# Two-sided decode attention: one whole-tile V slot and a mixed P·V product instead of two half slots

## The chip, the cores and the metric

The kernel runs on one core of a Trainium2 chip. The metric is device time in microseconds from one launch; a time here is the median of runs of the same program, and lower is better. The core has five engines: TensorE (PE, matrix products), VectorE (DVE, elementwise and reductions), ScalarE (ACT, activations), GpSimd (POOL) and SyncE (SP, here only a queue that issues loads). Sixteen DMA engines move data from HBM to on-chip memory.

## The reference

Two attention decode steps for a single token are computed side by side and concatenated. Each has 32 heads of 128, 32 key/value heads (no sharing), a cache of 16384 positions and a model width of 512, all in bfloat16.

```python
q = (x @ wq).reshape(B, Sq, Hq, Dh).transpose(0, 2, 1, 3)
scores = einsum("bhqd,bhkd->bhqk", q, k) * (Dh ** -0.5)
p = softmax(scores)
o = einsum("bhqk,bhkd->bhqd", p, v)
return o.transpose(0, 2, 1, 3).reshape(B, Sq, Hq * Dh) @ wo
```

Side A uses all 16384 positions of K and V. Side B uses the last 4096 of each head (a window). With one query row, every K and V element is read once and used once: 268 MB of K and V for A, 67 MB for B, and 17 MB of weights.

## The kernel before

**Steps.** The heads are worked through in 20 steps, `T` = 0 to 19, listed in `steps`. Sixteen belong to A (two heads each, 64 partitions per head, 256 positions per partition) and four, at `T` = 0, 7, 13 and 19, to B (eight heads in two windows of four heads, 128 positions per partition). Each step needs one K tile and one V tile of 128 partitions x 256 positions x 128, that is 64 KB per partition, 8.39 MB. Half a tile, 128 positions and 32 KB per partition, is called `u` = 0 or 1.

**Scores on VectorE.** `scores_prod` (L200) multiplies a half K tile by the query in place; `scores_tree` folds the 128 products of each position to 8 in four additions (L207) and reduces these to one score (L213). `unit_max` (L218, L220) takes the largest score per partition and turns it into a row by a PE transpose; `max_all` (L225, L229, L232) reduces that to a maximum per head and spreads it back over partitions.

**Softmax on ScalarE.** `soft` takes the exponential (L240), writes one copy of the probabilities per head masked to that head's partitions (`pm`, L248), and `soft_sum` and `recip` form the sums and their reciprocals.

**P·V on TensorE.** `pv` multiplies with the probabilities as the stationary operand, 8 or 16 columns wide, and 4 positions of V, 512 columns, as the moving one (L292): 64 matmuls per A tile. Row c of the result is good only in its own block of 128 columns. `evict` scales it to on-chip memory (L308), and `columns` picks the good blocks into columns with four small fp32 products (L323) and copies them into `O` (L327). Step NT - 3 and the last step use another form, `pv_columns` (L338): V itself is stationary, one position at a time, and the probabilities are 2 or 4 moving columns, so that the result is a column at once; `scale_columns` (L353) scales it on VectorE.

**Buffers and the order of loads.** Two pools hold the large tiles: `kring`, two slots of a whole K tile, and `vring`, two slots of half a V tile. SP issues nearly all loads, in program order, and waits in that order until the slot of a load is free. In step T it issues `load_v(T-1, 0)`, `load_k(T+1)`, and `load_v(T-1, 1)`; TensorE does `pv(T-2, 1)` and then `pv(T-1, 0)` in the same step. A's K rows are 64 KB, its V rows 32 KB; all of B's are 32 KB. At the start the two `wq` weights use the V slots; at the end the `wo` weights use a K slot and a V slot. The order of instructions on each engine is that of the program (`manual_schedule`): nothing is moved by a scheduler.

**Start.** `x` is loaded transposed, 128 partitions of 4 elements of 2 bytes (L417), and `spread_x` spreads it over masked columns; `project_q` forms the queries on PE.

**End.** `permute_o` reorders the columns of `O`. `project_out_rows` (L373) forms A's output with 32 matmuls of 512 columns. B's `wo` is loaded in four pieces (`wo_pieces`), and `project_out_columns` works them as they come: wo stationary for the first three (L393), and the last two rows of wo through `spread_o` with wo as the moving operand (L406). The result goes out from L412.

Of the kernel before, what the change touches and what calls it, by code (L numbers as in the profile page):

```python
# [11 lines left out]
P = 128  # L12
# [13 lines left out]
def kernel(  # L26
# [26 lines left out]
    vring = ctx.enter_context(tc.tile_pool(name="vring", bufs=2))  # L53
# [10 lines left out]
    def vslot(name):  # L64
        return vring.tile([P, CH, DH], BF16, tag="vring", name=name)
# [3 lines left out]
    one_f = singles.tile([1, 1], F32, tag="one_f")  # L69
    ones_col = singles.tile([P, 1], F32, tag="ones_col")  # L70
# [53 lines left out]
    def load_v(T, u, dst=None, pieces=1):  # L124
        s, g = steps[T]
        V[T, u] = vslot("vt") if dst is None else dst
        n = CH // pieces
        for k in range(pieces):
            if s is A:
                src = a_pair(A_v_cache, g)[:, u * CH : (u + 1) * CH, :].rearrange("p l d -> p (l d)")  # L130
            else:
                src = b_window(B_v_cache, 2 * g + u)
            nc.sync.dma_start(
                out=V[T, u][:, k * n : (k + 1) * n, :].rearrange("p l d -> p (l d)"),
                in_=src[..., k * n * DH : (k + 1) * n * DH],
            )

    def load_wq(s):
        s.wq_t = vslot("wqt")
        nc.sync.dma_start(  # L140
            out=s.wq_t[:, :, :].rearrange("p a b -> p (a b)").rearrange("p (c f) -> p c f", c=KC),
            in_=s.wq.rearrange("(p c) f -> p c f", c=KC),
        )
# [12 lines left out]

    def spread_x(s, flat):
        s.xb = flat[:, 0 : s.nh * KC * P].rearrange("p (h c m) -> p h c m", h=s.nh, c=KC)
        nc.vector.memset(s.xb, 0.0)
        for j in range(s.nh):  # L160
# [7 lines left out]
    def project_q(s):  # L168
        wq = s.wq_t[:, :, :].rearrange("p a b -> p (a b)").rearrange(
# [13 lines left out]
    class Unit:  # L183
        def __init__(self, T, u):
            self.T = T
            self.s, g = steps[T]
            self.col = self.s.nh * g if self.s is A else self.s.nh * (2 * g + u)
            self.n = 2 * CH if self.s is A else CH
            self.rows = 4 * self.s.nh
            self.split = T == NT - 3  # L190
            self.last = self.split or T == NT - 1
            self.sc = one.tile([P, 2 * CH], F32, tag="sc", name="sc")

# [8 lines left out]
    def scores_tree(T, u):  # L202
        s, g = steps[T]
# [5 lines left out]
        if s is B or u == 0:  # L209
            units[T, u] = Unit(T, u)  # L210
        un = units[T, u if s is B else 0]
        c0 = u * CH if s is A else 0
        nc.vector.tensor_reduce(out=un.sc[:, c0 : c0 + CH], in_=k[:, :, 0:8], axis=AX.X, op=ALU.add)  # L213
        return un if s is B or u == 1 else None

    def unit_max(un):
        m = small.tile([P, 1], F32, tag="m", name="m")
        nc.vector.tensor_reduce(out=m[:, :], in_=un.sc[:, 0 : un.n], axis=AX.X, op=ALU.max)  # L218
        un.sm = ps_m.tile([P, 512], F32, tag="sm", name="sm")
        nc.tensor.transpose(un.sm[0:1, 0:P], m[:, :], identf[:, :])  # L220

    def max_all(un):
        s = un.s
        M = small.tile([1, 4], F32, tag="M", name="M")
        nc.vector.tensor_reduce(  # L225
            out=M[:, 0 : s.nh], in_=by_head(s, un.sm[0:1, 0:P]), axis=AX.X, op=ALU.max
        )
        Mr = one.tile([1, P], F32, tag="Mr", name="Mr")
        nc.vector.tensor_copy(  # L229
            by_head(s, Mr[:, :]), M[:, 0 : s.nh].unsqueeze(2).broadcast_to([1, s.nh, P // s.nh])  # L230
        )
        nc.tensor.matmul(un.sm[:, 128:129], lhsT=Mr[:, :], rhs=one_f[:, :], start=True, stop=True)  # L232

    def soft(un):
        s = un.s
        bias = small.tile([P, 1], F32, tag="bias", name="bias")
        nc.scalar.activation(out=bias[:, :], in_=un.sm[:, 128:129], func=ACT.Copy, scale=-inv)  # L237
        p = one.tile([P, 2 * CH], BF16, tag="p", name="p")
        cs = small.tile([P, 1], F32, tag="cs", name="cs")
        nc.scalar.activation(  # L240
            out=p[:, 0 : un.n], in_=un.sc[:, 0 : un.n], func=ACT.Exp, scale=inv, bias=bias[:, :],
            accum_out=cs[:, :],
        )
        un.cs = cs
        pm = small.tile([P, 4 * CH], BF16, tag="pm", name="pm")
        un.pm = pm[:, 0 : un.n * s.nh].rearrange("p (i h c) -> p i h c", h=s.nh, c=4)
        for j in range(s.nh):
            nc.scalar.activation(  # L248
                out=un.pm[:, :, j, :], in_=p[:, 0 : un.n].rearrange("p (i c) -> p i c", c=4),
# [3 lines left out]
        if un.last:  # L253
            un.csm = small.tile([P, 4], F32, tag="csm", name="csm")
            nc.scalar.activation(
                out=un.csm[:, 0 : s.nh], in_=s.mask[:, :], func=ACT.Copy, scale=un.cs[:, :]
            )

    def soft_sum(un):
        s = un.s  # L260
        if un.last:
            nc.tensor.matmul(
                un.sm[:, 136 : 136 + s.nh], lhsT=ones_col[:, :].broadcast_to([P, P]),
                rhs=un.csm[:, 0 : s.nh], start=True, stop=True,
            )
        else:
            nc.tensor.matmul(
                un.sm[0 : un.rows, 136:137], lhsT=s.rows[:, :, :].rearrange("p a b -> p (a b)"),
# [264 lines left out]
```

## Time and profile before

| | |
|---|---|
| median of 3 runs | 828.04 us (827.94 to 828.24) |
| the profiled execution's own time | 828.17 us |
| its span, first to last instruction | 826.4 us |
| busy: DVE / PE / ACT | 761.6 / 387.3 / 67.1 us |
| moved by the load queue | 352.33 MB |
| mean rate over the span | 427 GB/s |
| mean granted TensorE clock | 0.704 of full |

The profile page gives busy time per engine, the load queues with the share of 16 engines' span that their packets took, and the chain of work that ended last: followed back from the last instruction, at each step to what released it. Lines of a timeline are: start in us, duration, engine, source line, operation, what it writes and reads, a count, and in brackets how long the engine was idle before and what ended that. PE is a matmul, PEld the loading of its stationary operand, SPq the issue of a load. Lines of windows give, for a stretch of time, its length, then the busy time and count of PE, PEld, DVE, ACT and POOL, then the granted TensorE clock, the DMA share, and GB/s.

### The profile page before, as it was taken

The page shows a single profiled execution, that of the slowest core. Times are in us where ns is not written, and L with a number is a line of the kernel's source. Part 1 is how long each engine was busy: PE and PEld are TensorE (multiplying, and loading weights), DVE is VectorE, ACT ScalarE, POOL GpSimd, SP SyncE. Part 2 cuts the span into 40 slices and gives each one's busy share as a digit, 9 for nine tenths or more (in the row PEclk, how much of TensorE's full clock was granted, in tenths as well). Part 3 has the DMA queues.
Part 4 walks back from the last instruction along what each step waited for, and adds up shares of the span by engine and source line. Part 5 has one row for each costly group of instructions (what it writes and reads, how often), then busy time and mean ns, then how long its engine had stood idle before and what let it go on. Part 6 is the DMA issues. An engine that isn't in the chain of part 4 may idle for free.

```text
span 826.4 us, 4998 instructions
## 1 busy us (share of the span) xinstructions
PE 387.3 (47%) x2100; PEld 172.3 (21%) x2100; DVE 761.6 (92%) x363; ACT 67.1 (8%) x194; POOL 0.7 (0%) x6
## 2 busy tenths in 40 slices
PE   3405062708172645536180817354453617180884
PEld 1101021303031212212030302121221203030444
DVE  1899999999999999999999999999999999999930
ACT  0110010101000001101010100010010101010110
POOL 0000000000000000000000000000000000000000
PEclk9766577768585858677675858586766767585695
DMA  9999999999999999999999999999999999999996
GB/s 381 431 431 432 429 435 428 435 427 438 446 416 431 431 446 420 440 423 437 423 439 430 437 425 431 440 428 446 416 444 420 447 416 447 415 431 431 429 424 289
DMA packets 10688, 352.64 MB, mean 427 GB/s; under 512 B 1449, under 2 KB 1450, under 8 KB 1706
## 3 DMA queue, kind: packets, MB, share of 16 engines
q1 hardware_dynamic: 10376, 352.33, 99.1%
q8 instruction: 16, 0.26, 0.1%
q10 hardware_dynamic: 290, 0.00, 0.0%
q14 instruction: 6, 0.05, 0.0%
HBM read 352.32 MB, written 0.00 MB: 426 GB/s over the span
## 4 chain that ended last, share of the span: by engine, by line
DVE 79%; DMA 18%; PE 2%; issue 1%; ACT 0%; DVEq 0%; ACTq 0%; SPq 0%
DVE kt L200 36%; DVE kt L207 35%; DMA kt<-in_A_k_cache_dram 10%; DVE sc L213 5%; DMA wot<-in_B_wo_dram 4%; DMA xTA<-in_A_x_dram 3%; DMA vt<-in_A_v_cache_dram 2%; PE o L292 1%; DVE m L218 1%; DVE Mr L229 1%; DVE M L225 0%; PE ocol L338 0%; PE out_cols L393 0%; DVE r L277 0%; PE out_rows L406 0%
## 5 line engine op out<-in xcount | busy, mean ns | idle before, releaser
L207 DVE TENSOR_TENSOR kt<-kt 128x8192 bf16<-128x8192 bf16 (+3 forms) x160 | 344.9, 2156 | 4.7
L292 PE MATMUL o<-vt,pm 128*8 128x512 bf16 (+1 forms) x1184 | 299.1, 419 | 0.4 <-DMA vt<-in_A_v_cache_dram 0.2
L200 DVE TENSOR_TENSOR kt<-kt,qA 128x16384 bf16<-128x16384 bf16 x32 | 277.5, 8672 | 2.8 <-DMA kt<-in_A_k_cache_dram 2.8
L292 PEld LDWEIGHTS <-pm 128*8 128x8 bf16 (+1 forms) x1184 | 110.1, 94 | 180.1 <-issue 58.6
L220 PE MATMUL sm<-identf,m 128*1 128x128 f32 x24 | 8.5, 355 | 201.5 <-DVE m L218 201.4
L232 PE MATMUL sm<-one_f,Mr 1*128 1x1 f32 x48 | 13.1, 340 | 176.1 <-DVE Mr L229 176.1
L200 DVE TENSOR_TENSOR kt<-kt,qB 128x16384 bf16<-128x16384 bf16 x8 | 69.4, 8681 | 0.0
L213 DVE TENSOR_REDUCE sc<-kt 128x128 f32<-128x1024 bf16 x40 | 48.8, 1220 | 2.9
L232 PEld LDWEIGHTS sm<-one_f,Mr 1*128 1x128 f32 x48 | 11.1, 285 | 183.1 <-DVE Mr L229 182.6
L220 PEld LDWEIGHTS sm<-identf,m 128*1 128x1 f32 x24 | 1.9, 79 | 204.1 <-issue 195.2
L237 ACT ACTIVATE bias<-sm 128x1 f32<-128x1 f32 x24 | 4.1, 171 | 405.1 <-PE sm L232 405.0
L308 ACT ACTIVATE o<-o,r 8x512 f32<-8x512 f32 (+1 forms) x21 | 14.2, 678 | 156.3 <-PE o L292 156.3
L323 PE MATMUL oc<-identf,o 8*128 8x2 f32 (+1 forms) x168 | 22.0, 249 | 2.9 <-ACT o L308 2.9
L323 PEld LDWEIGHTS oc<-identf,o 8*128 8x128 f32 (+1 forms) x168 | 20.2, 186 | 10.4 <-issue 6.5
L177 PE MATMUL qp<-wqt,scratch 128*128 128x512 bf16 x32 | 8.4, 429 | 13.8 <-DVE scratch L166 13.8
L248 ACT ACTIVATE pm<-p,maskA 128x256 bf16<-128x256 bf16 x32 | 14.5, 500 | 0.5
L177 PE MATMUL qp<-wqt,xbA 128*128 128x512 bf16 x32 | 8.9, 446 | 11.1 <-DMA wqt<-in_A_wq_dram 11.1
L353 DVE TENSOR_TENSOR OB<-ocol,r 128x4 bf16<-128x4 f32 x2 | 0.3, 162 | 13.0 <-PE ocol L338 13.0
L240 ACT ACTIVATE p<-sc,bias 128x256 bf16<-128x256 f32 (+1 forms) x24 | 11.3, 472 | 0.8
L327 ACT CAST OA<-oc 128x2 bf16<-128x2 f32 x15 | 2.4, 160 | 102.6 <-PE oc L323 102.6
L166 DVE COPY scratch<-xTB 128x128 bf16<-128x128 bf16 x4 | 0.7, 315 | 10.8 <-DMA xTB<-in_B_x_dram 10.8
L248 ACT ACTIVATE pm<-p,maskB 128x128 bf16<-128x128 bf16 x32 | 10.2, 390 | 0.3
(68 smaller groups left out, 105.2 us busy)
## 6 DMA issues: line engine op xcount, KB each, us to landing
vt<-in_A_v_cache_dram SPq DMA_DIRECT2D x32, 4096.0 KB, 26.6
kt<-in_B_k_cache_dram SPq DMA_DIRECT2D x8, 4096.0 KB, 31.8
vt<-in_B_v_cache_dram SPq DMA_DIRECT2D x7, 4096.0 KB, 30.2
wqt<-in_B_wq_dram SPq DMA_DIRECT2D x1, 4096.0 KB, 12.4
wqt<-in_A_wq_dram SPq DMA_DIRECT2D x1, 4096.0 KB
wot<-in_A_wo_dram SPq DMA_DIRECT2D x1, 4096.0 KB, 24.7
wot<-in_B_v_cache_dram SPq DMA_DIRECT2D x2, 2048.0 KB, 26.2
wot<-in_B_wo_dram SPq DMA_DIRECT2D x1, 2048.0 KB, 27.1
```

Source lines behind the costliest of these rows:

```text
L177: nc.tensor.matmul(qp[:, :, :], lhsT=s.xb[:, j, c, :], rhs=wq[:, c, j, g : g + 4, :], start=(k == 0), stop=(k == n - 1),)
L200: nc.vector.tensor_tensor(out=k, in0=k, in1=s.q[:, j : j + 1, :].broadcast_to([P, CH, DH]), op=ALU.mult)
L207: nc.vector.tensor_tensor(out=k[:, :, 0:w], in0=k[:, :, 0:w], in1=k[:, :, w : 2 * w], op=ALU.add)
L213: nc.vector.tensor_reduce(out=un.sc[:, c0 : c0 + CH], in_=k[:, :, 0:8], axis=AX.X, op=ALU.add)
L218: nc.vector.tensor_reduce(out=m[:, :], in_=un.sc[:, 0 : un.n], axis=AX.X, op=ALU.max)
L220: nc.tensor.transpose(un.sm[0:1, 0:P], m[:, :], identf[:, :])
L232: nc.tensor.matmul(un.sm[:, 128:129], lhsT=Mr[:, :], rhs=one_f[:, :], start=True, stop=True)
L240: nc.scalar.activation(out=p[:, 0 : un.n], in_=un.sc[:, 0 : un.n], func=ACT.Exp, scale=inv, bias=bias[:, :], accum_out=cs[:, :],)
L248: nc.scalar.activation(out=un.pm[:, :, j, :], in_=p[:, 0 : un.n].rearrange("p (i c) -> p i c", c=4), func=ACT.Copy, scale=s.mask[:, j : j ...
L292: nc.tensor.matmul(un.o[0 : un.rows, :], lhsT=un.pm[:, i0 + i, :, :].rearrange("p a b -> p (a b)"), rhs=V[T, u][:, 4 * i : 4 * i + 4, :], ...
L308: nc.scalar.activation(out=un.osb[0 : un.rows, :], in_=un.o[0 : un.rows, :], func=ACT.Copy, scale=un.r[0 : un.rows, 0:1],)
L323: nc.tensor.matmul(oc[:, 0 : s.nh], lhsT=un.osb[0:n, j * P : (j + 1) * P], rhs=sel[:, j, :], start=(j == 0), stop=(j == 3),)
```

## The change

V gets one slot of a whole tile instead of two of half a tile. A's V is loaded by one DMA per step with 64 KB rows, before the step's K load; B's V by two DMAs into the halves of the same slot.

A step's softmax and P·V are done in one piece instead of by halves. `pv` takes three quarters of the positions (of the tile for A, of each window for B) in wide matmuls with the probabilities stationary, copies that result out on ACT unscaled (`part`), takes the last quarter with V stationary in `pv_columns`, and adds the blocks of `part` to the same columns. `scale_columns` then scales on VectorE two steps after the scores, in every step. The sums come from `csm` and a matmul of ones in every step. B's two windows share one `unit_max`, `max_all` and `soft`.

`x` is loaded as a row of 512 on one partition and turned into columns by four matmuls (`turn_x`). In the last steps, V of step 19 goes into half of the K slot that also holds A's `wo`, and into half of the V slot that also holds B's `wo`; B's `wo` has five pieces, all worked with wo stationary, and `spread_o` is gone. The special form of step NT - 3 is gone too.

```diff
-    vring = ctx.enter_context(tc.tile_pool(name="vring", bufs=2))
+    vring = ctx.enter_context(tc.tile_pool(name="vring", bufs=1))
...
-        return vring.tile([P, CH, DH], BF16, tag="vring", name=name)
+        return vring.tile([P, 2 * CH, DH], BF16, tag="vring", name=name)
...
-    def load_v(T, u, dst=None, pieces=1):
+    def load_v(T):
         s, g = steps[T]
-        V[T, u] = vslot("vt") if dst is None else dst
+        V[T] = vslot("vt")
+        if s is A:
+            nc.sync.dma_start(
+                out=V[T][:, :, :].rearrange("p l d -> p (l d)"),
+                in_=a_pair(A_v_cache, g).rearrange("p l d -> p (l d)"),
+            )
+        else:
+            for u in (0, 1):
+                load_v_half(T, u, V[T][:, u * CH : (u + 1) * CH, :])
+
+    def load_v_half(T, u, dst, pieces=1):
+        src = b_window(B_v_cache, 2 * steps[T][1] + u)
         n = CH // pieces
         for k in range(pieces):
-            if s is A:
-                src = a_pair(A_v_cache, g)[:, u * CH : (u + 1) * CH, :].rearrange("p l d -> p (l d)")
-            else:
-                src = b_window(B_v_cache, 2 * g + u)
             nc.sync.dma_start(
-                out=V[T, u][:, k * n : (k + 1) * n, :].rearrange("p l d -> p (l d)"),
-                in_=src[..., k * n * DH : (k + 1) * n * DH],
-            )
-
-    def load_wq(s):
-        s.wq_t = vslot("wqt")
+                out=dst[:, k * n : (k + 1) * n, :].rearrange("p l d -> p (l d)"),
+                in_=src[:, :, k * n * DH : (k + 1) * n * DH],
+            )
...
+    def turn_x(s):
+        ps = ps_t.tile([P, KC], F32, tag="tp", name="xps")
+        for c in range(KC):
+            nc.tensor.matmul(
+                ps[:, c : c + 1], lhsT=s.x_row.rearrange("o (p c) -> o c p", c=KC)[:, c, :],
+                rhs=one_b[:, :], start=True, stop=True,
+            )
+        nc.vector.tensor_copy(s.xT[:, :], ps[:, :])
...
+        un.csm = small.tile([P, 8], F32, tag="csm", name="csm")
+        for v in range(un.parts):
             nc.scalar.activation(
-                out=un.csm[:, 0 : s.nh], in_=s.mask[:, :], func=ACT.Copy, scale=un.cs[:, :]
+                out=un.csm[:, v * s.nh : (v + 1) * s.nh], in_=s.mask[:, :], func=ACT.Copy,
+                scale=un.cs[:, v : v + 1],
             )
 
     def soft_sum(un):
-        s = un.s
-        if un.last:
-            nc.tensor.matmul(
-                un.sm[:, 136 : 136 + s.nh], lhsT=ones_col[:, :].broadcast_to([P, P]),
-                rhs=un.csm[:, 0 : s.nh], start=True, stop=True,
-            )
-        else:
-            nc.tensor.matmul(
-                un.sm[0 : un.rows, 136:137], lhsT=s.rows[:, :, :].rearrange("p a b -> p (a b)"),
-                rhs=un.cs[:, :], start=True, stop=True,
-            )
+        w = un.parts * un.s.nh
+        nc.tensor.matmul(
+            un.sm[:, 264 : 264 + w], lhsT=ones_col[:, :].broadcast_to([P, P]), rhs=un.csm[:, 0:w],
+            start=True, stop=True,
+        )
 
...
+    def pv(un):
+        s, n = un.s, un.rows
+        sel = identf[0:n, 0:n].rearrange("k (h c) -> k c h", c=4)
+        wide = un.n * 3 // 4
+        un.ocol = []
+        for v in range(un.parts):
+            l0 = v * un.n
+            o = ps_o.tile([16, 512], F32, tag="o", name="o")
+            for i in range(0, wide, 4):
+                nc.tensor.matmul(
+                    o[0:n, :],
+                    lhsT=un.pm[:, (l0 + i) // 4, :, :].rearrange("p a b -> p (a b)"),
+                    rhs=V[un.T][:, l0 + i : l0 + i + 4, :],
+                    start=(i == 0), stop=(i == wide - 4),
+                )
+            part = one.tile([16, 512], F32, tag="o4", name="part")
+            nc.scalar.copy(part[0:n, :], o[0:n, :])
+            oc = pv_columns(un, V[un.T], l0, wide, un.n, False)
             for j in range(4):
                 nc.tensor.matmul(
+                    oc[:, 0 : s.nh], lhsT=part[0:n, j * P : (j + 1) * P], rhs=sel[:, j, :],
                     start=False, stop=(j == 3),
                 )
+
+    def pv_columns(un, V_t, l0, a, b, whole=True):
+        s = un.s
+        oc = ps_s.tile([P, 4], F32, tag="sp", name="oc")
+        for l in range(a, b):
+            nc.tensor.matmul(
+                oc[:, 0 : s.nh], lhsT=V_t[:, l + (0 if whole else l0), :],
+                rhs=un.pm[:, (l0 + l) // 4, :, l % 4],
+                start=(l == a), stop=(whole and l == b - 1),
+            )
+        un.ocol.append(oc)
+        return oc
+
+    def scale_columns(un, v):
         s = un.s
         nc.vector.tensor_tensor(
+            out=s.O[:, un.col(v) : un.col(v) + s.nh], in0=un.ocol[v][:, 0 : s.nh],
+            in1=un.r[:, v * s.nh : (v + 1) * s.nh], op=ALU.mult,
         )
 
...
-    wo_pieces = (16, 10, 4, 2)
+    wo_pieces = (16, 8, 4, 3, 1)
     with tc.manual_schedule():
+        scratch = kslot("scratch")
+        x0 = 4 * KC * P
         for s in (B, A):
-            nc.scalar.dma_start(out=s.xT[:, :], in_=s.x[0, 0, :].rearrange("(p c) -> p c", c=KC))
-        scratch = kslot("scratch")
+            s.x_row = scratch[0:1, :, :].rearrange("p a b -> p (a b)")[:, x0 : x0 + D]
+            nc.scalar.dma_start(out=s.x_row, in_=s.x[0, 0:1, :])
+            x0 += D
         new_k(0)
-        load_wq(B)
+        wqt = vslot("wqt")
+        load_wq(B, wqt[:, 0:CH, :])
         load_k(0, 0)
-        load_wq(A)
+        load_wq(A, wqt[:, CH : 2 * CH, :])
...
+        for T in range(NT):
+            if T >= 1:
+                load_v(T - 1)
                 if T + 1 < NT:
                     new_k(T + 1)
                     load_k(T + 1)
+            if T == NT - 1:
                 W = kslot("wot")
                 load_wo(A, W[:, 0:CH, :], (HQ,))
+                load_v_half(T, 0, W[:, CH : 2 * CH, :])
+            scores_prod(T, 0)
+            if T >= 2:
+                for v in range(units[T - 2].parts):
+                    scale_columns(units[T - 2], v)
+            if T >= 1:
+                max_all(units[T - 1])
+                soft(units[T - 1])
+                soft_sum(units[T - 1])
+                pv(units[T - 1])
+            scores_tree(T, 0)
+            if T >= 1:
+                recip(units[T - 1])
+            scores_prod(T, 1)
+            scores_tree(T, 1)
+            unit_max(units[T])
+        Z = vslot("wot")
+        load_v_half(NT - 1, 1, Z[:, 0:CH, :])
+        load_wo(B, Z[:, CH : 2 * CH, :], wo_pieces)
+        un = units[NT - 1]
+        scale_columns(units[NT - 2], 0)
+        max_all(un)
         permute_o(A)
+        soft(un)
         project_out_rows(A)
+        soft_sum(un)
+        recip(un)
+        un.ocol = []
+        for v, Vh in enumerate((W[:, CH : 2 * CH, :], Z[:, 0:CH, :])):
+            pv_columns(un, Vh, v * CH, 0, CH)
+            scale_columns(un, v)
         permute_o(B)
         project_out_columns(B, wo_pieces)
 
 
...
```

## The prediction, made before the result was known

> **What bounds the kernel now.** I read the page first, its busy shares and DMA queues, then the chain of work that ended last in order of time, the timeline of the DMA-issuing queue, and the timeline around one P·V product and around the end.
>
> ```profile
> PE 387.3 (47%) x2100; PEld 172.3 (21%) x2100; DVE 761.6 (92%) x363; ACT 67.1 (8%) x194; POOL 0.7 (0%) x6
> ...
> q1 hardware_dynamic: 10376, 352.33, 99.1%
> ```
> ```profile
> 597.00:715.00 118.00, 55.05 (x232) 22.64 (x232) 113.85 (x50) 7.56 (x21) 0.00 (x0) 0.69 1.00 432
> ```
>
> Two resources are full at once. VectorE (DVE) has 92%, and the one load queue keeps all 16 DMA engines busy 99.1% of the span. The second line is a stretch of 118 us: the last columns are clock, DMA share and GB/s, so a saturated stream moves 432 GB/s, 9.7 us for a 4.19 MB half load and 19.4 us for a whole K or V tile. The middle of the kernel needs 8.39 + 8.39 MB a step, 38.8 us of stream; DVE's own step is 38.14 us (product starts at 425.29 and 463.43). DMA is the slower by a little.
>
> ```profile
> 675.11 39.77 DMA kt<-in_A_k_cache_dram
> 714.91 8.69 DVE kt L200
> ...
> 790.39 29.80 DMA wot<-in_B_wo_dram
> 820.24 1.23 PE out_cols L393 x40
> ```
> ```profile
> 656.77 7.41 SPq L133 DMA_DIRECT2D vt<-in_A_v_cache_dram  x2
> 675.11 0.33 SPq L113 DMA_DIRECT2D kt<-in_A_k_cache_dram  x1
> 696.63 7.24 SPq L133 DMA_DIRECT2D vt<-in_A_v_cache_dram  x2
> 713.89 1.19 SPq L119 DMA_DIRECT2D kt<-in_B_k_cache_dram  x2
> ```
>
> K18 takes 39.77 us from issue to use: about 1 us of K17, two V halves issued before it (2 x 9.7) and itself (19.4). So the queue is first in, first out, and what is issued ahead of a K delays it. V16's second half is issued after K18 (696.63), so it costs K18 nothing. DVE waits for K four times, from about step 15 on, and the end is DMA again: the last pieces of B's wo arrive at 820 to 822, and little follows.
>
> **The change, part by part.** S(T) is the start of DVE's step T, k(T) the landing of K(T).
>
> *Rows of 64 KB.* The trace's packet records give 1.2194 us to a 32 KB packet and 2.4244 us to a 64 KB one: two for one saves 0.0144 us, 8 per engine and load: 0.115 us for each A step, 1.85 us over 16. Engines have no holes between packets, so halving the number of loads brings nothing else.
>
> *One slot.* V(T) is now issued only when every matmul on V(T-1) is done, and the K behind it on SP waits too. What covers this is the K transfer after V(T-1) lands, 19.4 us. The path against it is P·V, semaphore, issue, first bytes.
>
> ```profile
> 416.85 16.85 PE L292 MATMUL o<-vt,pm 128*8 128x512 bf16 x64
> ...
> 417.23 0.13 PEld L292 LDWEIGHTS <-pm 128*8 128x8 bf16 x1 [0.30 <-issue]
> 417.66 0.13 PEld L292 LDWEIGHTS <-pm 128*8 128x8 bf16 x1 [0.30 <-issue]
> ...
> 422.75 10.45 PEld L292 LDWEIGHTS <-pm 128*8 128x8 bf16 x49 [0.27 <-issue]
> ```
> ```profile
> 763.85 3.57 PE L338 MATMUL ocol<-pm,vt 128*128 128x2 bf16 x128
> ```
>
> Wide matmuls start every 0.427 us while the granted clock is 0.50, for about 13 of them, then every 0.213 us: 13 x 0.427 + 35 x 0.213 = 13.0 us for 48. The 64 stationary-V matmuls take 3.57/128 = 0.028 us each, 1.8 us, though one LDWEIGHTS record is 0.104 us long. Semaphore to issue is 0.35 us, issue to use (transfer excluded) about 1.4 us by wq at the start (issued 0.73, used 13.2 after 4.19 MB). Sum 16.6 us, 2.8 us inside the cover: no hole in the stream, cost taken as nothing. Bounds: nothing, and 64 x 0.104 = 6.7 us for the columns, giving 21.5 us and a hole of 2.1 us in each of 16 steps (+34 us); I take the first, because row L338 is the same instruction. B's P·V can start with the first half of V and is done sooner.
>
> The page "TensorE: Matmul & The Clock Gate" of the Trainium skill (LDWEIGHTS) gives a weight load P/1.2 ns, 107 ns for 128 columns, which would put the sum near the upper bound; its section on Fast Weight Load reduces that for full 128-column bf16 weights, and the spacing of 0.028 us agrees with the reduced one.
>
> *Order of the stream.* Each K now has the whole V(T-1) ahead of it instead of leaving a half behind it: every K from the second step on lands 9.7 us later in the stream, while the total is unchanged. DVE waits for K from step 2 on and runs at the stream's 38.7 us. In the middle that is free, since the stream paces it anyway; at the end it is not, because DVE's last two steps and all after them follow the last K.
>
> *DVE, ACT, PE additions.* Scaling the columns moves to DVE: 0.12 us a step, hidden while 38.14 + 0.12 is under 38.7; without that cover 2 us. ACT gains a copy and the masked sums, idle 92% of the time; P is ready about 11 us into a step (13 for B), V lands at 19.4. The join (eight passes, 1.05 to 1.86 us) comes after the last reader of V, so it holds no DMA; it ends near 38 us, ahead of the next step's M, 8.6 us into that step.
>
> *x as rows.* DVE's first product could start at about 23.4 rather than 24.15, but K2 then stops DVE, so only the stream counts. Its tiny packets cost between nothing and 0.8 us; I take 0.2, as engines show almost no idle there.
>
> *The end.* K18 landed at 714.91; with V16's second half ahead of it +9.7, 14 A steps of 64 KB rows -1.6, start -0.2: S(18) = 722.8. Step 18 lasted 38.16, plus the scale 0.12: S(19) = 761.1. From the start of step 19 to its last maximum took 38.73 (753.07 to 791.80); one maximum and one M, Mr pair fewer (-0.63), a scale and a longer maximum more (+0.26): done at 799.45, against 791.80. Then comes a chain that lay behind the stream before:
>
> ```profile
> 791.51 0.29 DVE L218 TENSOR_REDUCE m<-sc 128x1 f32<-128x128 f32 x1
> ...
> 793.24 7.07 PE L373 MATMUL out_row<-wot,OpA 128*1 128x512 bf16 x32
> ...
> 814.05 0.16 DVE L353 TENSOR_TENSOR OB<-ocol,r 128x4 bf16<-128x4 f32 x1 [8.08 <-PE ocol L338]
> ...
> 815.20 0.19 ACT L368 CAST OpB<-op 128x32 bf16<-128x32 f32 x1 [0.35 <-PE op L364]
> ...
> 824.12 0.35 SPq L412 DMA_DIRECT2D out_dram<-rows  x1
> ```
>
> - Two transposes (0.37 cold each), M and Mr of 256 (0.4 each, as a maximum takes 0.28 over 128 and 0.42 over 256), two fp32 broadcasts (0.55 each), permuting A's output (1.1): 4.0 us (1.44 before, one part and a warm clock): 803.45.
> - A's output rows, 32 wide matmuls, 7.07 us warm. PE's previous work ends near 796; in the trace the clock is 0.50 again 1.5 to 4 us after PE stops. Bounds 7.0 warm, 13.7 all cold. Ramps in the trace last 2.3 to 5.8 us, mean 4.2: 9.7 x 0.427 + 22.3 x 0.219 = 9.0: 812.4.
> - Sum of exponentials 0.4; 256 columns in two runs of 3.5 = 7.0: 819.8 (V19's second half lands at about 810).
> - Scale to permuted B: 814.05 to 815.43, 1.4: 821.2. All 128 output matmuls at 0.029 (L393: 64 in 1.87) = 3.75: 825.0.
> - Reduce, transpose, copy, issue: 1.2 (822.12 to 824.12 less the eight removed matmuls): 826.2. The five wo pieces are in by 820 (822.1 less 2.1), so the stream no longer sets the end.
> - Issue to end of span 2.28: span 828.5.
>
> The same page (HAM clock gate) says one busy window of 3.4 us restores the full clock: 8 cold matmuls instead of 9.7, 0.35 us less at this place; the trace's ramps decide.
>
> The profiled execution took 828.17 with a span of 826.4: 1.77 around it, and 0.13 above the median. 828.5 + 1.77 - 0.13 = 830.1 us.
>
> **The rivals.** (1) *The single slot stops the stream.* For: two half slots let one half load while the other is used; DMA has no slack. Against: 2.8 us of margin. It decides once P·V exceeds about 17.6 us; each us over costs 16 us. Half a us over: 838; columns at 0.104: 864.
> (2) *Warm clock, or a shorter chain at the end.* A's output rows at 7.0 instead of 9.0: 828.1, no change that can be told.
> (3) *Faster: the stream still sets the end.* Then only the 1.85 of rows, 0.2 at the start and 0.25 of the last steps show: 825.7. It needs DVE's last maximum 4.5 us earlier, which happens if K18 lands by 718, that is if loads do not keep to order of issue. The 39.77 us speak against it.
> (4) *Rows do not matter at all*: 1.6 us onto the main sum, 831.7, inside its range.
>
> **How the numbers follow.** The end chain (with 4) 0.60, own range 828.5 to 832.5, of which 0.18 within 0.2%; rival 1 0.20; rival 2 0.09; rival 3 0.11. A measurement of this kernel tells 0.2%, 1.7 us, from no change. Slower 0.42 + 0.20 = 0.62, within 0.27, faster 0.11. The range runs from 827.0, which leaves out rival 3, to 838.0, which takes in the stalls of up to half a us a step and leaves out the rest, about 0.08.
>
> **What would show it.** In the new profile: a first-in-first-out queue still near 99%; DVE waiting for K in nearly every step, each 38.7 to 38.8 us; V issued about 15 us after P·V begins and before K has landed; DVE's last maximum at about 799; A's output rows starting near a clock of 0.50; B's output columns following without a wait for wo. Wrong if DMA slices drop below 0.97 (rival 1), if V's columns take over 0.04 us each, or if PE still waits for wo at the end (rival 3).

## The result, and the profile after

The changed kernel takes 833.89 us (median of 6 runs, 833.08 to 836.8) against 828.11 (6 runs, 827.94 to 828.26): a ratio of 1.0074, interval 1.0063 to 1.0085. It is slower, as forecast and inside the range, but by 5.8 us where 2.0 were forecast. The profiled execution took 834.76 us with a span of 833.0, 0.9 above the median.

From the page of the changed kernel, busy time per engine and the load queues:

```profile
PE 370.1 (44%) x2915; PEld 185.8 (22%) x2915; DVE 763.3 (92%) x366; ACT 61.2 (7%) x174; POOL 0.7 (0%) x6
...
q1 hardware_dynamic: 8072, 352.33, 98.5%
q8 instruction: 23, 0.38, 0.2%
```

DVE is as busy as before, and the stream still fills the DMA engines, though 98.5% is less than 99.1%. PE has 815 more matmuls, and a queue that the forecast never looked at, the one that fetches instructions, has 23 packets of 16 KB where the kernel before had 16.

The chain that ended last in the changed kernel, in order of time (start, duration, what):

```profile
686.95 39.46 DMA kt<-in_A_k_cache_dram
726.43 8.69 DVE kt L220
...
802.52 0.42 DVE m L237
...
806.69 9.70 PE out_row L365 x32
...
816.72 6.48 PE oc L334 x248
823.20 1.20 issue
824.39 0.39 PE oc L334 x8
...
826.19 3.57 PE out_cols L379 x128
```

In the kernel before, the last link was a DMA of B's wo. Now the chain runs from the landing of K18 through DVE's last two steps into PE's tail, with no load in it, as the main forecast had it. Three things in it are not as forecast: K18 lands at 726.43 and not at 722.8, A's output rows take 9.70 and not 9.0, and the 256 columns of V take 8.2 (816.57 to 824.76) and not 7.0, because PE stands for 1.20 us in the middle of them, waiting for nothing that the profile shows.

One step of P·V and the issue of the next V, from the timeline of the changed kernel:

```profile
473.01 12.75 PE L315 MATMUL o<-vt,pm 128*8 128x512 bf16 x48 [7.03 <-DMA vt<-in_A_v_cache_dram]
485.69 1.76 PE L334 MATMUL oc<-pm,vt 128*128 128x2 bf16 x64
487.48 0.33 SPq L129 DMA_DIRECT2D vt<-in_A_v_cache_dram  x1
...
492.43 8.69 DVE L220 TENSOR_TENSOR kt<-kt,qA 128x16384 bf16<-128x16384 bf16 x1 [0.59 <-DMA kt<-in_A_k_cache_dram]
```

From V's landing to the issue of the next V it is 14.5 us (forecast 15.2). The issue comes about 5 us before the K ahead of it is in use (487.48 against 492.43), and that looked safe.

The trace's packet records show what it did all the same. From 100 to 700 us the mean DMA engine stood empty for 1.0 us in all (before: none), and the mean 64 KB packet took 2.4351 us where it had taken 2.4244. The slow ones stand in groups where the engines come to a V just issued: single packets there take 0.2 to 1.5 us longer. Over 4,096 packets on 16 engines that is 2.7 us each, more than the 1.85 that the longer rows were to save.

The records also show why 5 us is little. Each load ends with a packet of 4 bytes on each of the 16 engines, and these do not come together: in the kernel before, K18's come between 711.02 and 714.46. A load has landed when its slowest engine is done, and by then the fastest has been without work for 3.4 us, unless the next load is already queued. In the changed kernel there are eleven steps between 120 and 700 us where an A step's V is issued and DVE then starts on the K ahead as soon as it has landed. In nine of them the fastest engine is done with that K 1.0 to 3.1 us after V's issue, and of the eleven, engines stand empty only in those where it is under 2.6.

### The profile page after: what moved, and what is told of

The parts are those of the page before. It is cut to its first block, busy times and chain, and to the rows that moved or that the text cites. A ratio compares the mean times of both kernels' runs of the same rounds, so it can differ in the third digit from the quotient of the medians.

```text
span 833.0 us, 6574 instructions
## 1 busy us (share of the span) xinstructions
PE 370.1 (44%) x2915; PEld 185.8 (22%) x2915; DVE 763.3 (92%) x366; ACT 61.2 (7%) x174; POOL 0.7 (0%) x6
## 3 DMA queue, kind: packets, MB, share of 16 engines
q1 hardware_dynamic: 8072, 352.33, 98.5%
## 4 chain that ended last, share of the span: by engine, by line
DMA 48%; DVE 48%; PE 3%; issue 1%; SPq 0%; ACT 0%; DVEq 0%
DMA kt<-in_A_k_cache_dram 43%; DVE kt L220 22%; DVE kt L226 22%; DMA kt<-in_B_k_cache_dram 5%; DVE sc L230 3%; PE out_row L365 1%; PE oc L334 1%; PE out_cols L379 0%; DVE M L255 0%; DVE Mr L257 0%; DVE Mr L259 0%; PE sm L261 0%; SPq L148 0%; DVE m L237 0%; DVE r L304 0%
## 5 line engine op out<-in xcount | busy, mean ns | idle before, releaser
L315 PE MATMUL o<-vt,pm 128*8 128x512 bf16 (+1 forms) x912 | 242.8, 434 | 115.2 <-DMA vt<-in_A_v_cache_dram 115.2
L315 PEld LDWEIGHTS <-pm 128*8 128x8 bf16 (+1 forms) x912 | 87.4, 96 | 261.0 <-issue 175.9
L322 ACT COPY part<-o 8x512 f32<-8x512 f32 (+1 forms) x22 | 12.7, 576 | 374.5 <-PE o L315 374.5
L334 PEld LDWEIGHTS <-vt 128*128 128x128 bf16 x1216 | 32.0, 96 | 9.5 <-issue 9.5
L334 PE MATMUL oc<-pm,vt 128*128 128x2 bf16 (+1 forms) x1216 | 33.9, 164 | 0.0
L296 PE MATMUL sm<-csm,ones_col 128*128 128x2 f32 (+1 forms) x40 | 11.6, 360 | 42.2 <-ACT csm L289 42.2
L269 ACT ACTIVATE bias<-sm 128x1 f32<-128x1 f32 (+1 forms) x20 | 3.4, 172 | 327.7 <-PE sm L261 327.7
L325 PE MATMUL oc<-identf,part 8*128 8x2 f32 (+1 forms) x176 | 23.5, 251 | 0.0
L325 PEld LDWEIGHTS oc<-identf,part 8*128 8x128 f32 (+1 forms) x176 | 21.6, 189 | 0.4
L296 PEld LDWEIGHTS sm<-csm,ones_col 128*128 128x128 f32 x40 | 9.8, 305 | 44.2 <-ACT csm L289 43.8
L282 ACT ACTIVATE pm<-p,maskA 128x256 bf16<-128x256 bf16 x32 | 14.5, 500 | 0.5
L195 PE MATMUL qp<-wqt,xbA 128*128 128x512 bf16 x32 | 9.4, 465 | 10.6 <-DMA wqt<-in_A_wq_dram 10.6
```

The costliest lines, as they stand in the source:

```text
L282: nc.scalar.activation(out=un.pm[:, :, j, :], in_=p[:, :].rearrange("p (i c) -> p i c", c=4), func=ACT.Copy, scale=s.mask[:, j : j + 1],)
L296: nc.tensor.matmul(un.sm[:, 264 : 264 + w], lhsT=ones_col[:, :].broadcast_to([P, P]), rhs=un.csm[:, 0:w], start=True, stop=True,)
L315: nc.tensor.matmul(o[0:n, :], lhsT=un.pm[:, (l0 + i) // 4, :, :].rearrange("p a b -> p (a b)"), rhs=V[un.T][:, l0 + i : l0 + i + 4, :], st ...
L322: nc.scalar.copy(part[0:n, :], o[0:n, :])
L325: nc.tensor.matmul(oc[:, 0 : s.nh], lhsT=part[0:n, j * P : (j + 1) * P], rhs=sel[:, j, :], start=False, stop=(j == 3),)
L334: nc.tensor.matmul(oc[:, 0 : s.nh], lhsT=V_t[:, l + (0 if whole else l0), :], rhs=un.pm[:, (l0 + l) // 4, :, l % 4], start=(l == a), stop= ...
```

## The experiments

All numbers are medians, with the ratio to the kernel before and its 95% interval. Five theories were tried: the order of the stream (each K a half V later), the one slot (a V issued just in time), the instruction fetches (more PE instructions, more packets of 16 KB on the engines that load), the chain at the end, and x.

**All of P·V with V stationary.** P·V is then meant to be short (7 us in place of 14.5), but PE has 5,475 matmuls.

```diff
-            for i in range(0, wide, 4):
-                nc.tensor.matmul(
-                    o[0:n, :],
...
-            oc = pv_columns(un, V[un.T], l0, wide, un.n, False)
+            pv_columns(un, V[un.T], v * un.n, 0, un.n, False)
```

> All of P.V with V stationary (256 matmuls of 0.028 us a step, no wide part, no join); all else as in the changed kernel. Theory 1 (V's load is issued so late that engines find their queue empty at the start of each V, and the first packets of a load that starts on an empty queue are slow): the slot is free 7.0 us after V lands instead of 14.5, V's load is queued well ahead, the stream gains back about 3 us by K18, 830.5 to 831.5 us. Theory 2 (rows of 64 KB are slower in themselves): no change, 833.9. Theory 3 (instruction fetches, 23 of 16 KB against 16 before, take the engines' time): more than twice the P.V matmuls, more fetches, slower by 1 to 3 us, 835 to 837.

Measured 836.59 us, 1.0104 (1.0089 to 1.0119); K18 at 727.86, 43 instruction fetches, a pause of 1.86 in the last columns. Two things happen at once. V is now issued 8 to 15 us ahead of K's use, no engine stands empty between 100 and 700 us, and the mean engine is done with K18 at 723.27 instead of 724.67. But 34 fetches instead of 17 come before K18, and its 16 engines are spread from 719.30 to 727.35 (changed kernel: 723.52 to 725.95), so that the slowest is 1.4 us later. P·V itself does not keep to 7 us either: in 17 steps PE stands for 1.2 to 3.9 us in the middle of the columns, waiting for nothing that the profile shows. A shorter path is not enough, and what this kernel has more of is instructions.

**All of P·V in wide matmuls.** The longest path, 16 to 17 us, and the fewest instructions.

```diff
-            for i in range(0, wide, 4):
+            for i in range(0, un.n, 4):
...
-            oc = pv_columns(un, V[un.T], l0, wide, un.n, False)
+            oc = ps_s.tile([P, 4], F32, tag="sp", name="oc")
```

> All of P.V in wide matmuls (64 a step for A), still in one slot. Theory 1: the slot is free about 1.9 us later than in the changed kernel, the first engines wait for each V that much longer; between +3 and +28 us (the last if every engine waits it out in each of 15 steps), 837 to 862. Theory 2: no change, 833.9. Theory 3: fewer instructions, 831 to 833.

Measured 838.89 us, 1.0131 (1.0115 to 1.0146), K18 at 731.62. The chain of this kernel has left DVE for the slot:

```profile
650.45 22.40 DMA vt<-in_A_v_cache_dram
672.90 15.68 PE o L314 x64
688.59 23.39 DMA vt<-in_A_v_cache_dram
712.02 16.58 PE o L314 x64
728.62 22.75 DMA vt<-in_A_v_cache_dram
```

A V lands, is used up in about 16 us, and the next lands some 23 us after its issue, of which 19.4 are its own: it was issued with 3 to 4 us of K left ahead of it. That is too late. The packet records show 4.3 us of empty engines from 100 to 700 us, and 2.4442 us for the mean 64 KB packet.

**A's V as two loads of 32 KB rows, both into the one slot.** The products and the slot are those of the changed kernel, but P·V can begin when the first half has landed.

```diff
-            nc.sync.dma_start(
-                out=V[T][:, :, :].rearrange("p l d -> p (l d)"),
-                in_=a_pair(A_v_cache, g).rearrange("p l d -> p (l d)"),
-            )
+            for u in (0, 1):
+                nc.sync.dma_start(
+                    out=V[T][:, u * CH : (u + 1) * CH, :].rearrange("p l d -> p (l d)"),
+                    in_=a_pair(A_v_cache, g)[:, u * CH : (u + 1) * CH, :].rearrange("p l d -> p (l d)"),
+                )
```

> A's V loaded into the same whole slot by two loads of 32 KB rows instead of one of 64 KB rows; P.V as in the changed kernel. Its wide part can start when the first half is in, 9.7 us earlier, so the slot is free about 9 us earlier against the stream. Theory 1: the 3 us come back, 830.5 to 831.5. Theory 2: back too, by 1 to 3 us. Theory 3: no change, 833.9. Together with the all-stationary run, which keeps the 64 KB rows, it tells 1 from 2.

Measured 834.0 us, 1.0071 (1.0056 to 1.0086). V is issued 8 to 14 us ahead of K's use instead of 4 to 10. The slow packets at the start of each V and the empty engines are gone (none from 100 to 700, K's 64 KB packets back at 2.4244), and so are the longer rows; K18 lands at 725.76, little earlier. The mean engine is done with it at 722.46, 2.2 us earlier than in the changed kernel, but the spread is 5.0 us instead of 2.4. Three of the steps up to K18 last 40.0 or 40.1 us where most last 38.8; what made the first two long stays open.

**Two 32 KB loads and P·V all wide, together.**

> The changed kernel with A's V in two loads of 32 KB rows and all of P.V in wide matmuls: half of P.V is done before the second half lands, so V's slot is free early, and there are few instructions (about 15 fetches). Theories 1 and 3 together: no slow first packets and as few fetches as before, K18 at 722 to 724 instead of 726.4, time 830 to 832. Theory 1 alone (fetches do not count): the same as the run with two halves and columns, 834.

Measured 830.73 us, 1.0032 (1.002 to 1.0043). Against the all-wide kernel only V's load was edited, and 8.2 us are gone; no engine stands empty between 100 and 700 us. But the edit moves the issue too, as P·V no longer waits for all of V. The issue of a V and the use of the K ahead of it, in the all-wide kernel, in this one, and in the all-stationary one:

```profile
493.35 0.33 SPq L129 DMA_DIRECT2D vt<-in_A_v_cache_dram  x1
496.34 8.69 DVE L220 TENSOR_TENSOR kt<-kt,qA 128x16384 bf16<-128x16384 bf16 x1 [0.40 <-DMA kt<-in_A_k_cache_dram]
```
```profile
479.54 0.81 SPq L130 DMA_DIRECT2D vt<-in_A_v_cache_dram  x2
490.06 8.69 DVE L221 TENSOR_TENSOR kt<-kt,qA 128x16384 bf16<-128x16384 bf16 x1 [0.48 <-DMA kt<-in_A_k_cache_dram]
```
```profile
482.17 0.33 SPq L129 DMA_DIRECT2D vt<-in_A_v_cache_dram  x1
492.81 8.69 DVE L220 TENSOR_TENSOR kt<-kt,qA 128x16384 bf16<-128x16384 bf16 x1 [0.63 <-DMA kt<-in_A_k_cache_dram]
```

That is 3.0, 10.5 and 10.6 us ahead. The third has 64 KB rows and no empty engines either, so the lead separates these kernels and the row size does not. No kernel issues 32 KB rows with a lead as short as 3 us, so what they would do there is not known.

Against the two-load kernel before it only P·V was edited, with 2,003 matmuls in place of 2,915 and 15 fetches in place of 23, and 3.3 us are gone: in the profiled executions 1.4 at K18 (724.37), 0.9 in A's output rows, whose clock fell differently (10.00 against 9.13), and 0.8 as the pause in the last columns is gone:

```profile
804.66 9.13 PE out_row L366 x32
...
814.10 6.54 PE oc L335 x256
```

**The kernel before with 128 tiny matmuls of constants in each of 18 steps.** They touch no tile that is loaded.

```diff
+    def tiny():
+        d = ps_t.tile([P, 4], F32, tag="tp", name="tiny")
+        for k in range(128):
+            nc.tensor.matmul(d[:, 0:2], lhsT=ident[:, :], rhs=ident[:, 0:2], start=(k == 0), stop=(k == 127))
```

> The kernel before, with 128 matmuls of 2 columns on constants (into a column nobody reads) added to each of 18 steps, after P.V, where PE would idle: 4600 PE instructions more, no wait moved. Theory 3 (instruction fetches take the load engines' time): 18 fetches of 16 KB more than the 16 before, about 1.5 us of one engine each, 1.7 us on the mean engine and up to 3 on the slowest: 829.5 to 831.5 us, with the load stream ending later by as much. Theory 1 (late issue of V): no change, 828.1.

Measured 832.45 us, 1.0051 (1.0036 to 1.0066), a little over what was expected of the fetches. From its page:

```profile
q1 hardware_dynamic: 10376, 352.33, 98.7%
q8 instruction: 34, 0.56, 0.3%
```

There are 18 more fetches, K18 lands 2.9 us later (717.79 against 714.91), and 0.7 us of stream is lost near 775 us, where V18's second half is issued 3 us later. In the packet records a fetch takes 1.07 us of one of the load engines, and the next load packet there is 0.5 us slower. Spread evenly, 18 of these make only 1.7 us; but they are not spread evenly. K18's fastest engine is done at 710.95 (before: 711.02), the mean one at 714.00 (712.53), the slowest at 717.25 (714.46), and the load has landed when the slowest is done: 1.5 us on the mean engine become 2.8 at the landing.

**A's output with wo stationary**, in the changed kernel: 128 matmuls of 3.57 us in place of 32 of 9.70.

```diff
-        project_out_rows(A)
+        project_out_columns(A, (HQ,), nc.scalar, 0)
```

> A's output formed with wo stationary (128 matmuls of 0.028 us = 3.6 us) instead of 32 wide matmuls that took 9.70 us at the end of the changed kernel; all else the same. If the chain after DVE's last maximum sets the end, it gets 6 us shorter until the stream's last wo piece (about 824.7 us) sets the end: 4 to 5 us faster than the changed kernel, about 829.3. If the stream sets the end already, no change, 833.9.

Measured 832.15 us, 1.0053 (1.0037 to 1.007): 6.1 us shorter at that place, 1.7 in the time. Its chain shows where the rest went:

```profile
804.66 3.57 PE out_cols L379 x128
...
809.07 0.60 PE oc L334 x23
809.67 1.86 issue
811.54 3.57 PE oc L334 x128
815.11 2.62 issue
817.73 2.98 PE oc L334 x105
```

Here PE stops after each 128 matmuls and their 128 weight loads, 256 instructions. The packet records, counted from the span's start, have fetches of 16 KB at 809.18 to 810.28 and 815.24 to 816.33: PE goes on 1.26 and 1.40 us after their ends. The next one, 821.21 to 822.23, is followed after 1.42 us by the end of a third pause, of 0.91. The fetches come 6 us apart, and PE uses 256 of these instructions in 3.57.

**One of the 32 matmuls of A's output rows**, first in the changed kernel, then in the kernel before.

```diff
-        for r in range(HQ):
+        for r in range(1):
```

> The changed kernel with 1 of the 32 matmuls of A's output rows; the other 31 are left out, so A's output is not formed. If the chain after DVE's last maximum sets the end, 9.3 us leave it until the stream's last wo piece sets the end: 4 to 5 us faster than the changed kernel, 829 to 830. If the stream sets the end already, no change, 833.9.

> The kernel before with one of the 32 matmuls of A's output rows; 31 of them are left out, so that only one row of wo counts. Theory that in the kernel before the end is set by the stream: these matmuls run beside the last loads (793 to 800 us, the last pieces of wo land at 820 to 822), so nothing is gained: 828.1 within 0.3, against the 4.3 us that the same cut gained in the changed kernel. Rival theory, that the chain after the last maximum counts in the kernel before too: 822 to 824.

The changed kernel came to 829.56 us, 1.0017 (1.0007 to 1.0027), 4.3 less; the kernel before to 828.05, 0.9999 (0.9989 to 1.0008), nothing. So these matmuls lay behind the stream and now lie on the path. In the changed kernel with one row the chain ends in a load again (this execution took 831.25, 1.7 above the median):

```profile
801.42 24.15 DMA wot<-in_B_wo_dram
825.62 0.62 PE out_cols L379 x16
```

This also bounds the gain: here the stream itself ends near 825.6, and in the kernel before its last packet was in by 822.

**x as rows**, alone, in the kernel before.

```diff
-            nc.scalar.dma_start(out=s.xT[:, :], in_=s.x[0, 0, :].rearrange("(p c) -> p c", c=KC))
+            nc.scalar.dma_start(out=s.x_row, in_=s.x[0, 0:1, :])
```

> The kernel before with x loaded as a row and turned by matmuls, as in the change; nothing else. The stream sets the end, so what the 8-byte packets cost comes off the whole. The prediction took 0.2 us; the changed kernel's second K half landed 0.8 us earlier than before: 827.3 to 827.9. If the packets of x cost nothing, 828.1.

Measured 827.46 us, 0.9992 (0.9982 to 1.0001): 0.65 less, three times the 0.2 of the forecast. The interval just takes in no change, but the slowest of these ten runs (827.77) is faster than the fastest of the kernel before beside them (827.87).

**The order of the loads alone**, in the kernel before: two half slots, 32 KB rows, the same instructions.

```diff
                 load_v(T - 1, 0)
                 if T + 1 < NT:
+                    load_v(T - 1, 1)
                     new_k(T + 1)
                     load_k(T + 1)
```

> The kernel before with the order of the loads alone changed: both halves of V(T-1) are issued ahead of K(T+1), and both halves of P·V of step T-1 run in step T. Two half slots, 32 KB rows of V, all products as before, the same number of instructions; in the last two steps P·V keeps its old places. Theory of the order (the main sum of the prediction): K18 lands half a V, 9.7 us, later, at 714.9 + 9.7 = 724.6, and DVE's last maximum comes at 791.8 + 9.7 = 801.5 instead of 791.8. Behind it 1.4 to A's output rows, 7.1 to 9.7 for these, 0.4, 7.1 for V's columns, 1.4, 3.5 of B's output columns, 2.0 to the issue, 2.3: a span of 826.7 to 829.3, so 828.3 to 830.9 us, most likely 830.2. V's loads begin without slow packets, as each half slot is free long before its turn, and the fetches stay at 16 or 17. Rival theory, that the order is harmless and all of the loss came from the one slot and the instructions: 828.1 within 0.4.

Measured 835.69 us, 1.0091 (1.0074 to 1.0108), more than either theory allowed. K18 landed at 724.43 (expected 724.6) and the last maximum came at 801.03 (801.5), so the order did to DVE what it was to do. But the issues of SyncE in this kernel show a second thing:

```profile
745.66 31.65 SPq L133 DMA_DIRECT2D vt<-in_A_v_cache_dram  x2
777.40 0.38 SPq L150 DMA_DIRECT2D wot<-in_A_wo_dram  x1
```

The second of the first two issues, V18's second half, came only at 777.0, behind columns of step 17 that stood behind the softmax of step 18, and the packet records have a hole of 7.4 us there. That hole comes from where this edit left those columns, not from the order; so the next kernel has them ahead of the softmax:

```diff
+            if x == 2 * NT - 2:
+                pv(T - 2, 1)
+                load_v(T - 1, 1)
             columns()
```

> The order of the loads alone, as in the run before it with this order, but with the columns of step 17's second half placed ahead of the softmax of step 18, as that run's one hole in the stream came from there: V(18,1) was issued at 776.97 us, after V(18,0) had landed at about 773, and it should now be issued at about 767, some 6 us ahead. Theory of the order: K18 at 724.4 and the last maximum at 801.0, as measured before; behind it, by the prediction's terms, 1.4, 9.0, 0.4, 7.1, 1.4, 3.5, 2.0, 2.3, so a span of 828.1 and 829.7 us; by the rows that were then measured (9.92 for A's output rows and 8.8 for V's columns, with a pause of 1.83 for instructions) 2.6 more, 832.3 us. So 829.5 to 832.5. Theory that the loss of 7.5 us in that run was the order itself and not the hole: 835 to 836. Rival theory, that the order is harmless: 828.1 within 0.4.

Measured 832.86 us, 1.0058 (1.0041 to 1.0074), 0.4 above the expected 829.5 to 832.5. The profiled execution is the fastest of the four, 831.82, against 832.86 to 832.94 for the others. From its page's queue lines, its chain and its timeline:

```profile
q8 instruction: 16, 0.26, 0.1%
```
```profile
684.70 39.77 DMA kt<-in_A_k_cache_dram
724.49 8.69 DVE kt L200
```
```profile
802.82 7.07 PE L373 MATMUL out_row<-wot,OpA 128*1 128x512 bf16 x32
...
813.28 1.10 PE L338 MATMUL ocol<-pm,wot 128*128 128x4 bf16 x38
...
816.77 2.54 PE L338 MATMUL ocol<-pm,wot 128*128 128x4 bf16 x90 [2.39 <-issue]
...
822.97 2.75 PE L393 MATMUL out_cols<-OpB,wot 128*128 128x1 bf16 x87 [1.21 <-issue]
```

The order alone makes the kernel before 4.8 us slower, with two slots, the old rows and 16 fetches. PE pauses twice in the tail, 3.6 us together, and in this execution that is nearly all of the 3.7 us lost: what the order does is to put PE's tail on the path, and the pauses there then count. What the other executions lost more was not profiled. The kernel before has the same columns, which come piece by piece behind loads, and its longest pause for instructions in them is 0.35. A smaller hole was left, 3.1 us near 790, where V19's first half waits for the wide matmuls on V18's; so the last wo landed at 825.1 to 825.8 as well, within 0.3 us of what PE alone would have needed.

**A version that beats both**: the kernel before with x as rows and the five pieces of wo of the change.

```diff
-    wo_pieces = (16, 10, 4, 2)
+    wo_pieces = (16, 8, 4, 3, 1)
...
-        spread_o(B, wo_pieces[-1])
```

> The kernel before with the two parts of the change that belong neither to the slot nor to the order: x as rows, and B's wo in five pieces (16, 8, 4, 3, 1), all with wo stationary and without the spread columns. Theory that the stream sets the end of this kernel: x as rows gains what it gained by itself, 0.65 us, and after the last piece 4 matmuls of 0.029 us, a reduction and a transpose take about 1.5 us, against 8 wide ones and a copy that took 2.0, so 827.0 to 827.6. Theory that the smaller pieces cost the stream as much as they save at the end: 827.3 to 828.1. If PE runs dry of instructions in these last columns too, as it did with 256 columns in a row: 0.4 to 1.2 us more than the first, 827.5 to 828.6.

Measured 826.74 us, 0.9983 (0.9974 to 0.9992): 1.4 us faster than the kernel before, 7.2 faster than the changed one, and a little below all that was expected. Its chain still ends in the stream:

```profile
791.90 29.12 DMA wot<-in_B_wo_dram
...
821.06 0.62 PE out_cols L397 x16
```

## Why the prediction was right and wrong

*What set the end* was right. The forecast's main case was that K comes a half V later, that this is free in the middle, and that DVE's last steps and the chain behind them then pass the stream. The one-row pair shows it (4.3 us in one kernel, nothing in the other), and the order alone puts K18 within 0.2 us of the sum's place for it. The signs named for it were there: DVE waits for K in nearly every step of A (13.0 us in all), the stream is full, V is issued some 15 us after P·V begins and before K has landed, and nothing in the tail waits for wo. Rival 3, that the stream still sets the end, fell with that; rival 2, a warm clock in A's output rows, would not have been enough, as the profiled execution of the order kernel had it warm and still lost 3.7 us.

*"One slot": "no hole in the stream, cost taken as nothing"* is the step that failed first. The path of P·V was sized well (14.5 us for 15.2) and stayed inside the cover of 19.4, but the bar was in the wrong place. The sum asks that V be issued before the slowest engine is done with K; the fastest is done some 2 to 3 us before that. With 5 us of K left ahead, V's issue already costs 1.0 us of empty engines and up to 2.7 of slow packets, with 3 to 4 us left 4.3 us of empty engines (the all-wide kernel), and with 8 us or more none. The rows' 1.85 us were therefore never seen; no run has the longer rows alone, with two slots. K18 was 3.6 us late; in the kernels that are the same program up to that point it was 1.6 late (A's output with wo stationary) and 4.3 late (one row), so this loss is not a fixed number. Rival 1 had the mechanism, as a hole that opens once P·V exceeds 17.6 us; it opens earlier, at 14.5, and gradually. The 64 stationary-V matmuls kept to the 0.028 us each that the sum took (1.76 us). That this "agrees" with the Fast Weight Load of the page cited there says too much: the page measures a gain of about two, which from 107 ns would be some 53 (an estimate), and the rows show 28.

*Missing from the sum: instructions.* The sum counted the 815 extra matmuls only as PE time. They also have to be fetched through the engines that load: 7 more fetches. The tiny matmuls show the price of such instructions where nothing else changes: 2.9 us at K18 for 16 more fetches ahead of it, 0.18 each. At that price the 6 more that the changed kernel has ahead of K18 are about 1.1 us, an estimate. Of the 3.3 us that the all-wide form gains with two loads, 0.9 are the clock and not the 8 fetches fewer.

*"256 columns in two runs of 3.5 = 7.0"* was mis-sized by 1.2 for the same reason. The duration came from runs of 128 columns before which PE had waited; that their instructions had arrived in those waits is argued, not shown. In an unbroken run of 28 ns pairs PE uses 256 instructions in 3.6 us. The pause is not certain: with two loads and P·V all wide the same 256 columns ran through in 6.54.

*A's output rows: 9.0 forecast, 9.70 measured*, which at 0.427 and 0.219 us each is 13 cold matmuls, not 9.7. The profiled execution of the order kernel has none. The Trainium skill, "TensorE: Matmul & The Clock Gate", HAM clock gate, says that the window runs freely and that one kernel measured 6, 11 or 14 cold matmuls; 13 and none are in keeping with a count that varies, and the 8 that one window of 3.4 us would give (an estimate) is not what this execution shows.

*x as rows* was worth 0.65 and not 0.2.

Forecast and measurement then differ by 3.8 us at the median. In the profiled execution the chain accounts for the 4.5 us by which its span is over the forecast one: 3.5 at the last maximum, 0.7 in A's output rows, 1.2 in V's columns, less 0.9 in the shorter links. By the experiments: the order +4.8 (with the pauses in its tail), x −0.65, and about +1.7 for slot, rows, fetches and tail together, where the sum had −1.85. That the parts add up so is an estimate; the tail's pauses fall differently in each kernel.

## What to carry to other kernels

A saturated queue needs its next load on it well ahead of the last byte of the one before, not just ahead of it, since its engines do not finish together; when a slot is taken away, look at how much is left in the queue at each issue, and count to the first engine that is done. Count added instructions twice where the DMA engines are full: as time on their engine, and as fetches on the engines that load. Take durations of long instruction runs from a row that is as long and as unbroken as the new one will be.

## What the runs showed that was not expected

- **PE can run out of instructions.** In runs of stationary-V or stationary-wo matmuls 12 of the 14 kernels have pauses of 0.3 us or more in which PE waits for nothing that the profile shows, 32 in all and up to 3.9 us long. Every one of them ends 1.2 to 1.6 us after a fetch of 16 KB has ended. The Trainium skill, "Runtime: NRT & Kernel Launch", Instruction fetch mechanics, gives blocks of 16 KiB, 256 instructions, and calls the cost of a boundary mostly hidden. The block agrees with the pauses that stand 256 instructions apart; hidden the cost was in the kernel with two loads and P·V all wide, and not in those with the pauses. What decides how far ahead the instructions are was not tried.
- **A load that is issued into a queue about to run empty starts slowly.** In the changed kernel 99 of 3,415 packets of 64 KB between 100 and 700 us took over 0.15 us longer than the usual 2.42, in the all-wide kernel 140, and 31 in the all-stationary one, whose loads are issued 8 to 15 us ahead and which has 31 fetches there. Why the first packets are slow was not tried, nor a short lead with 32 KB rows.
- **The same pause can leave PE's clock warm or cold.** In the two order kernels PE ends its wide matmuls 3.3 and 3.6 us before A's output rows start; these then took 9.92 us in the one and 7.07 in the other, the one with the longer pause. In the traces' clock records every stretch of one clock but the last is a multiple of 3.41 us long, and where these steps fall differs from run to run.
